# Routed experts of a fused attention and MoE kernel: late weight pieces behind evictions, early branch hints, gate products last, a third block's transposes inside the second's plan

## The chip, the cores and the metric

The kernel runs on one core of one Trainium2 chip. The metric is the device time of one launch in microseconds (us), the median of several runs. Each kernel is also profiled once; the times in the rows below are microseconds from the start of that profiled execution's span.

## The reference

Three stages follow each other on 1152 tokens (2 x 576) of 512 features:

1. Attention with 8 heads of 64 in which a token sees itself and the 63 before it.
2. A dense mixture of 4 experts: `out += p[:, e:e+1] * (relu(x @ w1[e]) @ w2[e])`, w1 512 x 1024, w2 1024 x 512.
3. A routed mixture of 8 experts, whose weights are other tensors. This is the stage that the change is about:

```python
skip_score = x @ w_skip
do_compute = skip_score > 0
out = x.copy()
xc = x[do_compute]
logits = xc @ w_gate
e_idx = np.argmax(logits, axis=1)
probs = np.exp(logits_s)
probs /= probs.sum(-1, keepdims=True) + 1e-09
gate_w = probs[np.arange(len(xc)), e_idx]
for e in range(E):
    mask = e_idx == e
    h = np.maximum(xc[mask] @ w1[e], 0.0)
    y[mask] = gate_w[mask, None] * (h @ w2[e])
out[do_compute] = xc + y
```

With the inputs used, 154 tokens are skipped, and experts 0 to 7 get 116, 207, 129, 66, 298, 17, 114 and 51. In blocks of 128 tokens: expert 0 has one; 1 has a second, full one; 2 has a second one with so few tokens that a small form (64 rows) serves; 3 has one; 4 has a full second and a small third one; 5 and 6 have one; 7 has a single small one.

## The kernel before, in words

Attention runs to about 90 us of the profile, the dense experts to about 488 us. Beside the last dense expert the routing is worked out tile by tile (nine tiles of 128 tokens, `route`, from L625 on): gate values, argmax, a running count, and products on PE (`tab`, L743) that collect each token's place, id and gate. From 488 us on the routed experts run one after the other, and the rest of this document is about them.

**An expert's block** (`block`, L885) works on 128 token rows. The rows are fetched from DRAM by an indirect DMA that POOL issues (`gather`, L851, tile `xg`; `xj` for a third block). `xpose` (L363 transposes on PE, then L878 on ACT and L880 on DVE) turns them and splits them into a high and a low part, `xs`. The first product (`g1`, two halves called g10 and g14 after their first chunk, matmuls L902) lands in PSUM as `mm`; in second and third blocks the PSUM tile is called `mmx`. ACT evicts it with the ReLU as `hr` (L926). PE transposes `hr` (L943), ACT and DVE split that into `ht` (L947, L950), and the second product (`g2`, L902 again) follows. DVE multiplies by the gate and adds to the token rows (L986, tile `xg`), and POOL scatters the rows to the output by an indirect DMA (`scatter`, L859). A `small` block does the same for 64 rows.

**Weights** come as eight pieces of 512 KB for each expert, four of w1 and four of w2, issued by SP (`w_load`, L315 for w1, L317 for w2) into a ring of `raw` buffers. ACT casts a piece to its high part (`wa1h`, `wa2h`, L331) and DVE subtracts for the low part (`wa1l`, `wa2l`, L335); the letters a and b are two sets of weight buffers used in turn, expert 0 having b and expert 1 having a. A raw buffer is free for the next load when both have read it.

**What sets the order.** The code does not issue instructions where it stands. `add(engine, duration, function, rd, wr, prio, slack)` gives an operation to `Plan`, and `plan.run()` sorts what has been collected: a list scheduler that walks along modelled times and takes, for each engine, the operation that is ready with the lowest `prio`; `slack` moves an operation's modelled readiness. The modelled times only set the order. On the chip every engine runs its own list in that order and waits at semaphores. So an operation that waits holds up all that stands behind it on its engine.

**Branches.** Counts are known only on the chip, so each expert's extra blocks stand behind branches, which every engine takes for itself: `more{e}` (L1105: are there more than one block?), the choice of the full or the small form (L1062), and the third block (L1095). Counters come into registers by three loads on each engine (`TENSOR_LOAD cnt x3`, L1052). On PE a hint (`ahead`, L1085) tells the sequencer ahead of time which way `more{e}` goes.

**Names that the steps use:** in `w_pass`, `w_split` of expert 1's w2; in `route`, `pick`, `rank` and `grab` (choice of the token rows of expert 0's first block, which come straight from SBUF by a product and not by a gather) and `spread` (the `tab` products); `route_gates`, which puts the gate products of the last tiles into the plan; `gather(e, 2)`, the rows of a third block; `rows` and `more`, which build the second and third blocks.

Of the kernel before, what the change touches and what calls it, by code (L numbers as in the profile page):

```python
# [204 lines left out]
def fused_kernel(ctx: ExitStack, tc: tile.TileContext, q, k, v, dp, w1, w2, wskip, wgate, m1, m2, out):  # L205
# [114 lines left out]
        add("X" if early else "SP", 0.0 if early else 1.46, f, rd=["M"] if extra else [], new=[b], prio=prio)  # L320
        return b

    def w_split(b, ring, key, part, c, prio, pool=False, after=(), hpool=False, hdve=False):
# [12 lines left out]

        add("POOL" if hpool else "DVE" if hdve else "ACT", 3.5 if hpool else c_dve(FF // 2) if hdve else c_act(FF, False), hi, rd=[b], wr=[(key, part, "h", c)], prio=prio)
# [285 lines left out]
    late, later = [], []  # L623

    def route(t):  # L625
        i = t % 2
        T = lambda nm: R[nm, i]
        K = lambda nm: ("r", nm, i)
        P = -5.0
        sl = 1.0 if t < TT - 1 else 0.0  # L630
        for d, nm in ((scr, "scr"), (out, "out")):
            add("SP", 0.8, lambda d=d: SP.dma_start(out=d[t * 128:(t + 1) * 128, :], in_=x2[:, t]),
# [77 lines left out]
            PE.matmul(out=first_at(kk), lhsT=x2[:, t, kk * 128:(kk + 1) * 128], rhs=rp.tile,  # L710
                      start=False, stop=(t == TT - 1), skip_group_check=True)

        if t > GT:
            rp = R["rpr"].buf()
            add("DVE", 0.35, pick, rd=["pf", K("oh"), "rconst"], new=[rp], prio=P)
        add("DVE", 0.2, rank, rd=["pf", K("oh")], wr=[K("ps")], prio=P + 0.5)
        if t > GT:
            for kk in range(KC):
                add("PE", 0.22, lambda kk=kk: grab(kk), rd=[rp, ("x2", t)], wr=[first[kk // 2]],
                    prio=P if t == TT - 1 else 3000.0)  # L720
            rp.close()

        def gate(c):
            sc, g, gb = T("sc"), T("g"), T("gb")
# [9 lines left out]
        def spread(c0, c1, pr, after=()):  # L734

            e0, n = c0 * E2, (c1 - c0) * E2
            wx = lambda: T("wy" if c0 else "wx")[:, :, 0:n]
            add("DVE", c_dve(TT * n) + 0.01, lambda: DVE.tensor_tensor(
                out=wx(),
                in0=T("w")[:, c0:c1].rearrange("p c e -> p (c e)").unsqueeze(1).to_broadcast([128, TT, n]),  # L740
                in1=T("oj").unsqueeze(2).to_broadcast([128, TT, n]), op=ALU.mult),
                rd=[K("oj")] + [K("w0")] * (c0 == 0) + [K("w1")] * (c1 == 5), wr=[K(("wx", c0))], prio=pr)
            add("PE", max(0.11, TT * n / 2400), lambda: PE.matmul(  # L743
                out=R["tab"].rearrange("p j c e -> p j (c e)")[:, :, e0:e0 + n], lhsT=T("r"), rhs=wx(),
                start=(t == 0), stop=(t in (GT, TT - 1)), skip_group_check=True),
                rd=[K("r"), K(("wx", c0)), *after], wr=[("tab", c) for c in range(c0, c1)], prio=pr, slack=sl)

        def gates(after=(), pr=2):
            for c in range(3):
# [2 lines left out]
        def weigh(after):  # L752
            add("DVE", 0.8, slot, rd=[K("ps"), *after], wr=[K("r"), K("oj")], prio=1)
            if t < TT - 2:
                gates()
                spread(0, 5, 2)
            else:
                spread(0, 2, 1)
                later.append(lambda: (gates(["idg", ("htl", 4)], 15), spread(2, 5, 15, ["idg"])))

        late.append(weigh)
        if t != TT - 2:
# [122 lines left out]
    def block(e, j, xg, x, small=False, amid=None):  # L885
# [46 lines left out]
        def tr(c0, w, hr):  # L932
            p = pt_r.buf()
            s = slice(c0, c0 + w)
            n = 64 if small else 128

            def turn():
                for g in range(w):
                    h = hr[:, 128 * g:128 * g + 128]
                    if small:  # L940
                        PE.matmul(out=p[:, g, 0:64], lhsT=h, rhs=fold2, start=True, stop=True)
                    else:
                        PE.transpose(out=p[:, g, :], in_=h, identity=ident)  # L943
# [6 lines left out]
            add("DVE", c_dve(w * n), lambda: DVE.scalar_tensor_tensor(  # L950
                out=ht[:, s, n:2 * n], in0=p[:, 0:w, 0:n], scalar=0.0, in1=f32(ht[:, s, 0:n]), op0=ALU.max,
                op1=ALU.subtract),
                rd=[p, ht, (ht, "h", c0)], wr=[(ht, "l", c0), ("htl", c0)], prio=-1)
            p.close()

        hrs = [g1(*pieces[0])]
# [37 lines left out]
    def w_pass(kd, e, p, prio=None):  # L994
        if prio is None:
            npass[0] += 1
            prio = 500.0 + 10 * npass[0]
        src = ((w1, w2) if kd == "m" else (m1, m2))[p - 1][e]
        ring, key = (wa, "wa") if kd == "m" else (rings[e], rkey[e % 2])
        for c in range(4):  # L1000
            extra = kd == "r" and e > 0 and p == 2
            st = KN["w2s"] if (kd, e, p) == ("m", 0, 2) else 2.5
            b = w_load(src, p, c, prio + st * c, extra, early=kd == "r" and e > 2 and p == 1)
            w_split(b, ring, key, p, c, prio + st * c, pool=(kd, e, p) == ("m", 0, 2) and KN["w2pool"][c],
                    after=["idg"] if kd == "r" and e == 1 else [])

    with tc.manual_schedule():
        w_pass("m", 0, 2, KN["w2p"])
        for e in range(E1):
# [28 lines left out]
            if e + 1 < E1:  # L1038
                w_pass("m", e + 1, 2)
        route_end()  # L1040
        add("X", 0.0, open_moe2, rd=["pf"], wr=["M"] + [("x2", t) for t in range(TT)] + [(x, f) for x in ("hh", "hl") for f in range(FC)], slack=-0.43)
        xgs, xts = {}, {}
        for j in range(2):
# [15 lines left out]
        def rows(e, j, x, xt):  # L1059

            state = [(b, b.left, b.closed) for b in (x, xt)], [(r, len(r.free)) for r in Ring.made]
            with tc.If(over(e, 2 * j + 1)) as c:  # L1062
                block(e, j, x, xt)
                if j == 0:
                    ahead(e)
                scatter(e, j, x)
                plan.run()
            with c.Else():
                for b, left, closed in state[0]:
                    b.left, b.closed = left, closed  # L1070
                for r, n in state[1]:
                    r.free = [0.0] * n
                block(e, j, x, xt, small=True)
                if j == 0:
                    ahead(e)
                scatter(e, j, x, 64)
                plan.run()

        def further(e):

            return nv[2] > 0 if e == E2 - 1 else over(e, 2)

        def hint(e):

            tc.mark_branch_hint_location(f"more{e}", hint=further(e), engines=[PE.engine, POOL.engine] if e == E2 - 1 else [PE.engine])  # L1085

        def ahead(e):
            if e:
                add("PE", 0.05, lambda: hint(e), rd=[("g2", 0)], wr=[("g2", 1)], prio=10.0)
            else:  # L1090
                add("PE", 0.05, lambda: hint(e), rd=["nv", ("g10", 1)], wr=[("g10", 2)], prio=10.0)

        def more(e, xt):
            for j in (1, 2):
                with tc.If(over(e, 4)) if j == 2 else ExitStack():  # L1095
                    if j == 2 and e == E2 - 1:
                        xgs[e, j] = gather(e, j)
                    if j == 2 or xt is None:
                        xt = xpose(xgs[e, j], 0)
                        plan.run()  # L1100
                    rows(e, j, xgs[e, j], xt)

        def tails(e, xt):

# [26 lines left out]

        for e in range(E2):
            last = e == E2 - 1
            if not last:
                xgs[e, 2] = gather(e, 2, 7, [("g2", 0)])
            if last:
                plan.run()
                rows(e, 0, xgs[e, 0], xts[e, 0])
                tails(e, None)
                continue  # L1140
            block(e, 0, xgs[e, 0], xts[e, 0], amid=None if e else route_gates)
            if e == 0:
                add("X", 0.0, counts, rd=["cnt"], wr=["nv"], slack=1.5)
            ahead(e)
# [43 lines left out]
```

## Time and profile before

| | us |
|---|---|
| median of 3 runs | 661.92 (660.07 to 665.22) |
| the profiled execution: its own time | 666.29 |
| the profiled execution: its span | 664.5 |
| PE busy | 631.3 (95% of the span) |
| DVE, ACT, POOL busy | 322.6, 235.9, 89.1 |

The mean granted clock of PE is 0.983 of full speed. PE is a matrix engine whose busy time is modelled from pipelined matmuls, so 95% is not 95% of its peak. The stage that the change touches begins at about 488 us. In the rows of the trace, a bracket at the end of a row is idle time of that engine just before the instruction and what released it; "issue" there is time in which the engine waited for nothing that the profile shows; PEq is PE's sequencer.

### The profile page before, as it was taken

To read this page: it belongs to the slowest core of one execution; us is meant where nothing else is said; L and a number is where in the kernel's file an instruction comes from. 1 tells how busy PE (TensorE), PEld (TensorE's weight loads), DVE (VectorE), ACT (ScalarE), POOL (GpSimd) and SP (SyncE) were. 2 spreads that over 40 slices of the span, in tenths; PEclk is the share of its full clock that TensorE was granted. 3 is DMA by queue.
4 is the path that set the end of the run, shared out by engine and by line. 5 is a ranking of instruction groups with operands and counts; after the bars stand their busy time and mean duration, and the time that the engine had idled before them with its cause. 6 is when DMAs were issued, how large, how long until landed. Compare 5 with 4: busy or idle time off the path is not lost. (4 is left out here: it accounts for less than half of the span.)

```text
span 664.5 us, 9657 instructions
## 1 busy us (share of the span) xinstructions
PE 631.3 (95%) x3652; PEld 556.0 (84%) x3652; DVE 322.6 (49%) x700; ACT 235.9 (36%) x492; POOL 89.1 (13%) x111
## 2 busy tenths in 40 slices
PE   7899999999999999999999999999968999999984
PEld 6787898898989898989898988989856878787764
DVE  5996841127412124412124426255657855862861
ACT  4974750125302013301013302113413764753741
POOL 6541130000000000000000000000023321320510
PEclk9998999999999999999999999999997999999988
DMA  9767200006400003400004401020538976990820
GB/s 218 163 160 224 47 4 0 1 1 211 169 1 0 1 1 126 127 1 0 1 1 127 127 32 65 14 83 12 191 122 309 314 228 215 295 332 19 245 100 11
DMA packets 55770, 71.40 MB, mean 107 GB/s; under 512 B 32938, under 2 KB 32938, under 8 KB 55697
## 3 DMA queue, kind: packets, MB, share of 16 engines
q1 hardware_dynamic: 52912, 62.17, 29.7%
q0 software_dynamic: 2784, 8.28, 4.0%
q8 instruction: 42, 0.69, 0.4%
q14 instruction: 32, 0.25, 0.1%
HBM read 63.74 MB, written 7.47 MB: 107 GB/s over the span
## 5 line engine op out<-in xcount | busy, mean ns | idle before, releaser
L523 PE MATMUL mm<-xth,wa1h 128*128 128x384 f32 (+1 forms) x416 | 138.0, 332 | 0.0
L523 PE MATMUL mm<-xtl,wa1h 128*128 128x384 f32 (+1 forms) x416 | 135.8, 326 | 0.0
L523 PE MATMUL mm<-xth,wa1l 128*128 128x384 f32 (+1 forms) x416 | 135.7, 326 | 0.0
L529 ACT ACTIVATE hh<-mm 128x384 fp32r<-128x384 f32 (+1 forms) x104 | 48.5, 467 | 236.3 <-PE mm L523 227.7
L544 PE MATMUL mm<-wa2h,hh 128*128 128x512 f32 (+1 forms) x296 | 116.8, 395 | 0.0
L544 PE MATMUL mm<-wa2h,hl 128*128 128x512 f32 (+1 forms) x296 | 115.0, 388 | 0.0
L544 PE MATMUL mm<-wa2l,hh 128*128 128x512 f32 (+1 forms) x296 | 114.9, 388 | 0.0
L531 DVE SCALAR_TENSOR_TENSOR hl<-mm,hh 128x384 fp32r<-128x384 f32 (+1 forms) x104 | 54.5, 525 | 123.2 <-ACT hh L529 123.2
L523 PEld LDWEIGHTS mm<-xth,wa1h 128*128 128x128 f32 x416 | 78.9, 190 | 0.7
L523 PEld LDWEIGHTS mm<-xtl,wa1h 128*128 128x128 f32 x416 | 78.8, 189 | 0.5
L523 PEld LDWEIGHTS mm<-xth,wa1l 128*128 128x128 f32 x416 | 78.7, 189 | 0.0
L544 PEld LDWEIGHTS mm<-wa2h,hl 128*128 128x128 f32 x296 | 55.7, 188 | 12.3
L544 PEld LDWEIGHTS mm<-wa2l,hh 128*128 128x128 f32 x296 | 55.8, 189 | 11.0
L544 PEld LDWEIGHTS mm<-wa2h,hh 128*128 128x128 f32 x296 | 55.8, 188 | 11.0
L556 DVE SCALAR_TENSOR_TENSOR x<-mm,prob,x 128x512 f32<-128x512 f32 (+1 forms) x28 | 20.5, 732 | 91.3 <-PE mm L544 91.3
L767 POOL DMA_INDIRECT x<-scr,id x1 | 1.3, 1252 | 360.2 <-DVE id L784 360.2
L331 ACT CAST wa2h<-raw 128x1024 fp32r<-128x1024 f32 x32 | 33.2, 1048 | 29.0 <-PE mm L544 18.6
L335 DVE TENSOR_TENSOR wa1l<-raw,wa1h 128x1024 fp32r<-128x1024 f32 x31 | 36.6, 1219 | 4.4 <-ACT wa1h L331 2.0
L335 DVE TENSOR_TENSOR wa2l<-raw,wa2h 128x1024 fp32r<-128x1024 f32 x30 | 35.9, 1218 | 5.2 <-ACT wa2h L331 5.0
L331 ACT CAST wa1h<-raw 128x1024 fp32r<-128x1024 f32 x30 | 30.0, 1049 | 13.0 <-DMA raw<-in_moe_w_dram 5.1
L950 DVE SCALAR_TENSOR_TENSOR ht<-pt,ht 128x512 fp32r<-128x512 f32 (+2 forms) x27 | 15.1, 569 | 31.3 <-ACT ht L947 27.6
L444 POOL TENSOR_TENSOR s<-s,mx 128x512 f32<-128x512 f32 x18 | 20.2, 1122 | 51.7 <-DVE mx L441 40.5
(206 smaller groups left out, 921.2 us busy)
## 6 DMA issues: line engine op xcount, KB each, us to landing
raw<-in_moe_w_dram SPq DMA_DIRECT2D x96, 512.0 KB, 5.5
scr<-x SPq DMA_DIRECT2D x9, 256.0 KB, 2.1
out_dram<-x SPq DMA_DIRECT2D x9, 256.0 KB, 2.3
qn<-in_q_dram SPq DMA_DIRECT2D x8, 256.0 KB, 4.0
kn<-in_k_dram SPq DMA_DIRECT2D x8, 256.0 KB, 3.9
vn<-in_v_dram SPq DMA_DIRECT2D x8, 256.0 KB, 4.7
qn<-in_q_dram SPq DMA_DIRECT2D x2, 128.0 KB, 4.6
kn<-in_k_dram SPq DMA_DIRECT2D x2, 128.0 KB, 4.7
```

Of the source, the lines that this page charges most:

```text
L331: (POOL.tensor_copy if hpool else DVE.tensor_copy if hdve else ACT.copy)(out=aps()[0], in_=b.tile)
L335: (POOL if pool else DVE).tensor_tensor(out=l, in0=b.tile, in1=f32(h), op=ALU.subtract)
L444: add("POOL", 1.0, lambda: POOL.tensor_tensor(out=s.tile, in0=s.tile, in1=mx[:, 3].unsqueeze(2).to_broadcast([128, HP, 128]), op=ALU.mult) ...
L523: PE.matmul(out=ps[:, 0:n], lhsT=wa[a][:, kk, f * 128:(f + 1) * 128], rhs=x[:, kk, g0:g0 + n], start=(i == 0), stop=(i == 3 * KC - 1))
L529: add("ACT", c_act(n), lambda: ACT.activation(out=hh[:, f, 0:n], in_=ps[:, 0:n], func=ACTF.Relu), rd=[ps], wr=[("hh", f)], prio=-1)
L531: add("DVE", c_dve(n), lambda: DVE.scalar_tensor_tensor(out=hl[:, f, 0:n], in0=ps[:, 0:n], scalar=0.0, in1=f32(hh[:, f, 0:n]), op0=ALU.max ...
L544: PE.matmul(out=ps[:, 0:c1 - c0], lhsT=x[:, f, o:o + 128], rhs=wa[a][:, f, c0:c1], start=(f == 0 and i == 0), stop=(f == FC - 1 and i == 2))
L556: DVE.scalar_tensor_tensor(out=z, in0=y, scalar=prob[:, t, e:e + 1], in1=z, op0=ALU.mult, op1=ALU.add)
L767: add("POOL", 1.0, lambda: POOL.indirect_dma_start(out=R["x0"], out_offset=None, in_=scr[0:128 * (GT + 1), :], in_offset=bass.IndirectOffs ...
L950: add("DVE", c_dve(w * n), lambda: DVE.scalar_tensor_tensor(out=ht[:, s, n:2 * n], in0=p[:, 0:w, 0:n], scalar=0.0, in1=f32(ht[:, s, 0:n]), ...
```

## The change

Four parts, all in the routed stage and what leads to it.

1. Expert 1's w2 pieces get `slack=7.0` on ACT, and the low parts of its w1 no longer have to follow the routing's index table (`idg`); only those of w2 do.
2. The choice of token rows of the next to last tile is put after the last tile's rows are there (`mid`), the gate products of the routing have no longer to follow a part of expert 0's block (`htl`) but get PE priority 21, and `route_gates` is called after `route_end` and not from inside expert 0's block.
3. `ahead`: the hint of every expert now follows the second group of g10; before, only expert 0's did, and the others' followed the first group of g2. In expert 1's and later blocks it stands 38 rows ahead of the branch on PE; before, 13.
4. The third block's rows are gathered after the first block's next gathers, and its transposes are put into the plan of the full second block (`amid`, prio 11.5); the branch to the third block stands inside that of the second's full form.

```diff
-    def w_split(..., hdve=False):
+    def w_split(..., hdve=False, slack=0.0):
...
-        add(... "ACT" ..., hi, rd=[b], wr=[(key, part, "h", c)], prio=prio)
+        add(... "ACT" ..., hi, rd=[b], wr=[(key, part, "h", c)], prio=prio, slack=slack)
...
+        while mid:
+            mid.pop()([("x2", t)])
...
-        if t > GT:
-            rp = R["rpr"].buf()
-            add("DVE", 0.35, pick, rd=["pf", K("oh"), "rconst"], new=[rp], prio=P)
-        add("DVE", 0.2, rank, rd=["pf", K("oh")], wr=[K("ps")], prio=P + 0.5)
...
+        def choose(after=()):
...
+        if t == TT - 2:
+            mid.append(choose)
+        else:
+            choose()
...
-                rd=[K("r"), K(("wx", c0)), *after], wr=[("tab", c) for c in range(c0, c1)], prio=pr, slack=sl)
+                rd=[K("r"), K(("wx", c0)), *after], wr=[("tab", c) for c in range(c0, c1)], prio=pe or pr, slack=sl)
...
-                later.append(lambda: (gates(["idg", ("htl", 4)], 15), spread(2, 5, 15, ["idg"])))
+                later.append(lambda: (gates(["idg"], 15), spread(2, 5, 15, ["idg"], 21)))
...
-                    after=["idg"] if kd == "r" and e == 1 else [])
+                    after=["idg"] if kd == "r" and e == 1 and p == 2 else [], slack=7.0 if kd == "r" and e == 1 and p == 2 else 0.0)
...
         route_end()
+        route_gates()
...
+            def gathered():
+                if e == E2 - 1:
+                    xgs[e, 2] = gather(e, 2)
+                third["xt"] = xpose(xgs[e, 2], 11.5)
             with tc.If(over(e, 2 * j + 1)) as c:
-                block(e, j, x, xt)
+                block(e, j, x, xt, amid=gathered if j == 1 else None)
...
                 plan.run()
+                if j == 1:
+                    with tc.If(over(e, 4)):
+                        rows(e, 2, xgs[e, 2], third["xt"])
...
         def ahead(e):
-            if e:
-                add("PE", 0.05, lambda: hint(e), rd=[("g2", 0)], wr=[("g2", 1)], prio=10.0)
-            else:
-                add("PE", 0.05, lambda: hint(e), rd=["nv", ("g10", 1)], wr=[("g10", 2)], prio=10.0)
+            add("PE", 0.05, lambda: tc.mark_branch_hint_location(f"more{e}", hint=further(e), engines=[PE.engine]),
+                rd=[("g10", 1)] + ["nv"] * (e == 0), wr=[("g10", 2)], prio=10.0)
...
-            for j in (1, 2):
-                with tc.If(over(e, 4)) if j == 2 else ExitStack():
...
+            if xt is None:
+                xt = xpose(xgs[e, 1], 0)
+                plan.run()
+            rows(e, 1, xgs[e, 1], xt)
...
-            if not last:
-                xgs[e, 2] = gather(e, 2, 7, [("g2", 0)])
...
-            block(e, 0, xgs[e, 0], xts[e, 0], amid=None if e else route_gates)
+            block(e, 0, xgs[e, 0], xts[e, 0])
+            xgs[e, 2] = gather(e, 2, 7, [("g2", 0)])
```

Line numbers of the changed kernel are higher by 10 from `block` on (L902 is L912, L926 is L936), and the branches' lines are L1120 (`more`), L1080 (full or small) and L1087 (third block).

How the order of instructions moves at three places:

On ACT, in expert 0's block, before; L926 evicts expert 0's hidden rows, `wa2h` casts are those of expert 1's w2.

```order
L878 CAST xs<-mm 128x256
L331 CAST wa2h<-raw_4175 128x1024
L926 ACTIVATE hr<-mm 128x512
L331 CAST wa2h<-raw_4195 128x1024
L1052 TENSOR_LOAD cnt x3
L947 ACTIVATE ht<-pt 128x4x128
L926 ACTIVATE hr<-mm 128x512
L331 CAST wa2h<-raw_4209 128x1024
L947 ACTIVATE ht<-pt 128x4x128
L331 CAST wa2h<-raw_4228 128x1024
L878 CAST xs<-pt 128x512 x2
```

The same place on ACT after the change:

```order
L888 CAST xs<-mm 128x256
L936 ACTIVATE hr<-mm 128x512
L1063 TENSOR_LOAD cnt x3
L957 ACTIVATE ht<-pt 128x4x128
L936 ACTIVATE hr<-mm 128x512
L957 ACTIVATE ht<-pt 128x4x128
L331 CAST wa2h<-raw_4180 128x1024
L888 CAST xs<-pt 128x512 x2
L331 CAST wa2h<-raw_4199 128x1024
L331 CAST wa2h<-raw_4212 128x1024
L331 CAST wa2h<-raw_4231 128x1024
```

The two evictions and the two `ht` parts, which stood behind one to three casts, now stand ahead of all four.

On POOL, expert 1's first block, before: gathers for later blocks (`xg`), for a third block (`xj`), the scatter and the branch `more`.

```order
L851 DMA xj<-scr,idg 128x512
L851 DMA xg<-scr,idg 128x512 x2
L859 DMA out_dram<-xg,ids 1152x512
L1105 REGISTER_ALU
L1105 COMPARE_AND_BRANCH
```

And after the change:

```order
L861 DMA xg<-scr,idg 128x512 x2
L861 DMA xj<-scr,idg 128x512
L869 DMA out_dram<-xg,ids 1152x512
L1120 REGISTER_ALU
L1120 COMPARE_AND_BRANCH
```

The third block's gather has moved from the first place to the third; so it has in the blocks of experts 2 to 6, while expert 0's order (six `xg`, then `xj`) stays.

On PE, from the end of expert 1's first block into its second, before (third-block transposes stand ahead of the third block, behind the branch of L1095):

```order
L902 MATMUL mm<-wa2h,ht 128x512 x4
L1105 REGISTER_ALU
L1105 COMPARE_AND_BRANCH
L1062 REGISTER_ALU
L1062 COMPARE_AND_BRANCH
L902 MATMUL mmx<-wa1h,xs 128x512
L902 MATMUL mmx<-wa1l,xs 128x512
L902 MATMUL mmx<-wa1h,xs 128x512
L902 MATMUL mmx<-wa1l,xs 128x512
L902 MATMUL mmx<-wa1h,xs 128x512
```

And after:

```order
L912 MATMUL mm<-wa2h,ht 128x512 x4
L1120 REGISTER_ALU
L1120 COMPARE_AND_BRANCH
L1080 REGISTER_ALU
L1080 COMPARE_AND_BRANCH
L912 MATMUL mmx<-wa1h,xs 128x512
L912 MATMUL mmx<-wa1l,xs 128x512
L912 MATMUL mmx<-wa1h,xs 128x512
L912 MATMUL mmx<-wa1l,xs 128x512
L363 MATMUL pt<-ident,xj 128x128 x4
L912 MATMUL mmx<-wa1h,xs 128x512
```

The four transposes of `xj` now stand behind the fourth matmul of the full second block, in every expert that has one.

## Rows read from the trace of the kernel before

**Rows 1.** Waits of PE, 488 to 664 us: total us, times, longest us.

```profile
PE pt L943 <- ACT hr L926: 5.5, 2, 4.8
PE mm L902 <- DVE wa2l L335: 2.9, 1, 2.9
PE mm L902 <- PEq L1105: 1.7, 2, 0.9
```

**Rows 2.** Windows around gaps of PE: length, then busy time of each engine.

```profile
core 0: us, PE busy (x) PEld busy (x) DVE busy (x) ACT busy (x) POOL busy (x), PEclk, DMA share, GB/s
...
493.55:498.38 4.83, 0.01 (x1) 0.01 (x1) 1.23 (x1) 1.60 (x3) 3.59 (x3) 1.00 0.96 311
498.56:505.39 6.83, 6.14 (x19) 4.65 (x19) 3.63 (x5) 4.36 (x6) 4.63 (x4) 0.50 1.00 361
600.58:602.82 2.24, 0.73 (x6) 0.42 (x5) 1.44 (x2) 0.61 (x1) 0.88 (x1) 1.00 0.00 0
639.74:642.74 3.00, 0.15 (x2) 0.04 (x1) 2.82 (x3) 0.00 (x0) 1.74 (x1) 0.86 0.03 8
642.74:648.75 6.01, 6.01 (x20) 5.27 (x21) 0.20 (x1) 0.98 (x2) 0.00 (x0) 0.50 0.12 42
```

**Rows 3.** PE's timeline in expert 0's block: start, us, instruction, idle before.

```profile
498.38 1.02 PE L943 MATMUL pt<-ident,hr 128*128 128x128 f32 x4 [4.83 <-ACT hr L926]
...
510.97 1.09 PE L902 MATMUL mm<-wb2h,ht 128*128 128x512 f32 x4
512.21 0.47 PE L902 MATMUL mm<-wa1h,xs 128*128 128x512 f32 x1
```

**Rows 4.** ACT's timeline in expert 0's block.

```profile
496.78 1.04 ACT L331 CAST wa2h<-raw 128x1024 fp32r<-128x1024 f32 x1 [8.19 <-DMA raw<-in_moe_w_dram]
```

**Rows 5.** DVE's timeline behind its three counter loads.

```profile
495.11 1.23 DVE L335 TENSOR_TENSOR wa1l<-raw,wa1h 128x1024 fp32r<-128x1024 f32 x1 [1.77 <-issue]
```

**Rows 6.** POOL's timeline: gathers and scatters, experts 0, 1, 3 and 4.

```profile
494.18 0.96 POOL L851 DMA_INDIRECT xg<-scr,idg  x1 [33.49 <-DVE idg L796]
495.45 1.70 POOL L851 DMA_INDIRECT xg<-scr,idg  x1 [0.30 <-issue]
497.45 0.95 POOL L851 DMA_INDIRECT xg<-scr,idg  x1 [0.31 <-issue]
...
513.64 1.75 POOL L859 DMA_INDIRECT out_dram<-xg,ids  x1 [9.39 <-DVE xg L986]
...
519.62 1.37 POOL L851 DMA_INDIRECT xg<-scr,idg  x1 [0.55 <-DMA out_dram<-xg,ids]
521.29 0.95 POOL L851 DMA_INDIRECT xg<-scr,idg  x1 [0.30 <-issue]
...
575.53 1.74 POOL L859 DMA_INDIRECT out_dram<-xg,ids  x1 [6.83 <-DVE xg L986]
...
582.43 0.94 POOL L851 DMA_INDIRECT xg<-scr,idg  x1 [2.60 <-DMA out_dram<-xg,ids]
```

**Rows 7.** DMA issues of 494.18; 495.45 and 521.29; 582.43 and 497.45; 632.74: landing us.

```profile
xg<-scr,idg POOLq DMA_INDIRECT x1, 7.4
...
xg<-scr,idg POOLq DMA_INDIRECT x1, 7.6
...
xg<-scr,idg POOLq DMA_INDIRECT x1, 8.3
...
xj<-scr,idg POOLq DMA_INDIRECT x1, 4.5
```

**Rows 8.** PE's timeline: first matmuls of the second blocks, experts 1 and 4.

```profile
525.37 0.40 PE L902 MATMUL mmx<-wa1h,xs 128*128 128x512 f32 x1
...
588.69 0.39 PE L902 MATMUL mmx<-wb1h,xs 128*128 128x512 f32 x1
```

**Rows 9.** PE's timeline: first matmul of expert 4.

```profile
575.40 0.49 PE L902 MATMUL mm<-wb1h,xs 128*128 128x512 f32 x1 [0.94 <-PEq L1105]
```

**Rows 10.** DVE's timeline: the last rows before expert 7 begins on PE.

```profile
640.59 2.35 DVE L335 TENSOR_TENSOR wa2l<-raw,wa2h 128x1024 fp32r<-128x1024 f32 x2
```

More of the change, by code (lines that the diff above doesn't have):

```diff
@@ L321, in w_load, with w_split @@
         return b
-    def w_split(b, ring, key, part, c, prio, pool=False, after=(), hpool=False, hdve=False):
+    def w_split(b, ring, key, part, c, prio, pool=False, after=(), hpool=False, hdve=False, slack=0.0):
         def aps():
@@ L335, in lo @@
             (POOL if pool else DVE).tensor_tensor(out=l, in0=b.tile, in1=f32(h), op=ALU.subtract)
-        add("POOL" if hpool else "DVE" if hdve else "ACT", 3.5 if hpool else c_dve(FF // 2) if hdve else c_act(FF, False), hi, rd=[b], wr=[(key, part, "h", c)], prio=prio)
+        add("POOL" if hpool else "DVE" if hdve else "ACT", 3.5 if hpool else c_dve(FF // 2) if hdve else c_act(FF, False), hi, rd=[b], wr=[(key, part, "h", c)], prio=prio, slack=slack)
         if pool:
@@ L621, in route_loads @@
         SP.dma_start(out=R["wr"][:, :, E2], in_=wskip.rearrange("(k p) -> p k", p=128))
-    late, later = [], []
+    late, later, mid = [], [], []
     def route(t):
@@ L711, in grab @@
                       start=False, stop=(t == TT - 1), skip_group_check=True)
-        if t > GT:
-            rp = R["rpr"].buf()
-            add("DVE", 0.35, pick, rd=["pf", K("oh"), "rconst"], new=[rp], prio=P)
-        add("DVE", 0.2, rank, rd=["pf", K("oh")], wr=[K("ps")], prio=P + 0.5)
[L717 to L721, printed above, removed]
+        def choose(after=()):
+            nonlocal rp
+            if t > GT:
+                rp = R["rpr"].buf()
+                add("DVE", 0.35, pick, rd=["pf", K("oh"), "rconst", *after], new=[rp], prio=P)
+            add("DVE", 0.2, rank, rd=["pf", K("oh"), *after], wr=[K("ps")], prio=P + 0.5)
+            if t > GT:
+                for kk in range(KC):
+                    add("PE", 0.22, lambda kk=kk: grab(kk), rd=[rp, ("x2", t)], wr=[first[kk // 2]],
+                        prio=P if t == TT - 1 else 3000.0)
+                rp.close()
+        rp = None
+        if t == TT - 2:
+            mid.append(choose)
+        else:
+            choose()
         def gate(c):
@@ L732, in gate, with spread @@
                 DVE.tensor_tensor(out=g[:, c + 1:c + 2], in0=g[:, c:c + 1], in1=gb[:, c:c + 1], op=ALU.subtract)
-        def spread(c0, c1, pr, after=()):
+        def spread(c0, c1, pr, after=(), pe=None):
             e0, n = c0 * E2, (c1 - c0) * E2
@@ L952, in tr @@
                 op1=ALU.subtract),
-                rd=[p, ht, (ht, "h", c0)], wr=[(ht, "l", c0), ("htl", c0)], prio=-1)
+                rd=[p, ht, (ht, "h", c0)], wr=[(ht, "l", c0)], prio=-1)
             p.close()
@@ L1061, in rows @@
             state = [(b, b.left, b.closed) for b in (x, xt)], [(r, len(r.free)) for r in Ring.made]
+            third = {}
+            def gathered():
+                if e == E2 - 1:
+                    xgs[e, 2] = gather(e, 2)
+                third["xt"] = xpose(xgs[e, 2], 11.5)
             with tc.If(over(e, 2 * j + 1)) as c:
-                block(e, j, x, xt)
+                block(e, j, x, xt, amid=gathered if j == 1 else None)
                 if j == 0:
@@ L1077, in rows @@
                 plan.run()
+            if j == 1:
+                M["xj"].free = [0.0] * M["xj"].n
         def further(e):
             return nv[2] > 0 if e == E2 - 1 else over(e, 2)
-        def hint(e):
-            tc.mark_branch_hint_location(f"more{e}", hint=further(e), engines=[PE.engine, POOL.engine] if e == E2 - 1 else [PE.engine])
         def ahead(e):
-            if e:
-                add("PE", 0.05, lambda: hint(e), rd=[("g2", 0)], wr=[("g2", 1)], prio=10.0)
-            else:
-                add("PE", 0.05, lambda: hint(e), rd=["nv", ("g10", 1)], wr=[("g10", 2)], prio=10.0)
+            add("PE", 0.05, lambda: tc.mark_branch_hint_location(f"more{e}", hint=further(e), engines=[PE.engine]),
+                rd=[("g10", 1)] + ["nv"] * (e == 0), wr=[("g10", 2)], prio=10.0)
         def more(e, xt):
-            for j in (1, 2):
-                with tc.If(over(e, 4)) if j == 2 else ExitStack():
[L1096 to L1101, printed above, removed]
+            if xt is None:
+                xt = xpose(xgs[e, 1], 0)
+                plan.run()
+            rows(e, 1, xgs[e, 1], xt)
         def tails(e, xt):
```

## The prediction

> **What bounds the kernel now.** I read the page first: PE is busy for 631.3 us of the 664.5 us span, so only time in which PE stands still, or runs at the lower clock, can be won. Then I asked for PE's waits in the routed part alone, 488 to 664 us [rows 1]. Three items matter: 5.5 us for hidden rows that ACT evicts (one wait of 4.8), 2.9 us put down to a DVE pass, 1.7 us for PE's own sequencer at the branch to an expert's second block. Third, a table of those stretches [rows 2]. [...] At half the clock a stretch in which PE is busy throughout (6.01 of 6.01) does what takes half as long at the full one, so it gives away about 3.0 us.
>
> The profiled execution took 666.29 us (span 664.5 and 1.8 around it), 4.4 above the median of 661.92. I add the differences below, worked out inside it, to the median.
>
> **Expert 0's block: ACT's order.** The 4.83 us gap ends with PE's transposes at 498.38 [rows 3]; they wait for hr, which ACT evicts behind a cast that itself stood 8.19 us for a weight transfer and ran from 496.78 on [rows 4]. The eviction had nothing else to wait for: PE's own work ended at 493.55 [rows 2]. After the change it runs at once. Expert 1 begins at 512.21 now [rows 3]. What goes: the 4.83 gap, about 3.3 us of lower clock behind it, and the second wait for hr, 5.5 - 4.8 = 0.7 [rows 1]: together 8.8.
> What comes instead: the three reads of counters on PE, which the long gap covers today, stand free (0 at best; DVE's wait at the same three reads is 1.77 [rows 5]; I take 1.5, near that row). And the eight transposes of gathered rows (xg) stand before the last matmuls of g2. PE would reach them at about 500.2, but the first two gathers are issued at 494.18 and 495.45 [rows 6] and take 7.4 and 7.6 us to land [rows 7]: 501.6 and 503.05. A new wait of 2.9 us, in two pieces. The last xg transposes, two gate products, eight matmuls of g2 and the branch are left: 2.65 (from 510.97 to 512.21, [rows 3], go the last four matmuls and the branch, 1.24; the rest I set at 1.4 by that row's pace, 1.09 for four). Expert 1 begins at 503.05 + 2.65 = 505.7, **6.5 earlier**. Nothing reaches higher, since the gathers' issue does not move. The low end: w1 raw buffers come free earlier, so SP issues up to 1.5 MB more in this stretch; at the 361 GB/s of [rows 2] that is 4.2 us of traffic, and if all of it came ahead of the gathers, the gain would be 2.3. I take 6.5, since gathers later in the program, with loads around them, still take 7.6 to 8.3 [rows 7].
> [...]
>
> **Expert 1: the third block's transposes.** Expert 1 has 207 tokens: two blocks, no third one. PE now meets four transposes of xj after four matmuls of the second block, whether or not a third follows. The chain up to xj is POOL's: scatter of expert 0's first block, its landing (which frees xg's buffer), two xg gathers, then xj, third where it was first. Today the scatter is issued at 513.64, 1.4 after expert 1 begins, and the first gather behind it at 519.62 [rows 6], 6.0 later. After: scatter at about 507.4 (its own rows land at about 505.7, then a DVE pass), gathers at 513.4 and 515.1, xj at 516.3, landed at 523.9 with the 7.6 of [rows 7]. PE is there at 505.7 + 13.2 (512.21 to 525.37, [rows 3, 8]) + 0.9 = 519.8. It stands for **4.1 us**, and its fifth matmul comes at about 524.6 instead of 526.3. Of the 6.5 only 1.7 is left. Bounds: with the shortest gather in the trace, 4.5 us [rows 7], the wait is 1.0; with 8.3 it is 4.8. I take 7.6, a gather of this very pair. A gap of 4.1 us is nearer to 4.83 and 3.00 than to 2.24, so I charge a lower stretch, 3.0 us (0 to 3.4).
>
> **Expert 4.** Here the second block is full and the third is real. The gap of 2.24 us between them, with transposes and splits [rows 2], goes. But the same chain decides: the scatter of expert 3 is issued at 575.53, the first xg gather at 582.43, when it has landed [rows 6]; the second and xj follow at 1.27 us each (as 494.18 and 495.45 do), 584.97, and xj lands 8.3 later [rows 7], at 593.27. PE is there at 588.69 + 0.9 = 589.6 [rows 8]: a wait of 3.7, and with the transposes (0.5) the fifth matmul comes 4.2 later than now. Net **+2.0**, and once more 3.0 for the clock (gap 4.2). With a gather of 4.5 there would be no wait and a gain of 1.6. The matmuls behind are PE-bound, so nothing gives this back.
>
> **Hints and branches.** The hint goes from 13 rows ahead of its branch to 38. Expert 0's hint already stood about 32 ahead, and behind it PE goes from 512.06 to 512.21 without a wait [rows 3]; with a late one the wait is 0.94 [rows 9], the other of [rows 1] 0.8. Of the two, the one before expert 4 is swallowed by expert 4's chain, which the scatter sets (0); the one before expert 6 gives **0.6**. Before expert 7 PE jumps twice in a gap of 3.00 us, to 642.74 [rows 2]. The waits put it down to DVE's wa2l [rows 1], but the passes of that name end at 640.59 + 2.35 = 642.94 [rows 10], 0.2 after PE has started, and expert 7's first matmul doesn't read wa2l. I take it for the jumps: **0.8** off, a gap of 2.2, and like the 2.24 one no lower clock behind it: **3.0** (0 if it stays). One branch fewer behind a small second block and one jump more behind the third cancel; each is bounded by the 0.94 of [rows 9].
>
> **Sum:** -1.7 + 3.0 (expert 1) + 2.0 + 3.0 (expert 4) - 0.6 - 0.8 - 3.0 = +1.9: 668.2 for the profiled execution, **664** for the median. The trace can tell some 1% (7 us; the three runs spread over 5).
>
> **Rivals.**
> B, the gathers of xj come in time: for it speaks the 4.5 us of one xj gather; against it that all gathers in a group of three took 7.4 to 8.3. Then expert 1's wait is 1.0 and without lower clock: -6.5 + 1.0 + 0.6 = -4.9; expert 4 gains 1.6 and keeps the 0.8 of its hint; with -0.6 - 0.8 - 3.0 that is -11.7: 650.
> C, slower: the earlier loads of w1 do get in the way of the first two gathers. At 361 GB/s for at most 1.5 MB they land up to 4.2 later; with 3.8, the stand before the xg transposes grows from 2.9 to 6.7, longer than the gap that brought the lower clock, and everything behind, expert 1's chain too, moves with it: +1.9 + 3.8 + 3.0 = +8.7: 671. It decides from 1.7 us of delay on if the clock falls there (1.9 + 1.7 + 3.0 = 6.6, 1%), from 4.7 if not. For it: the DMA share is already 1.00 in that stretch [rows 2].
> D, the early hints do nothing: the gaps at branches stay, the 0.6, 0.8 and 3.0 are not won, 1.9 + 4.4 = +6.3: 668. For it speaks that the target lies far off and many instructions are fetched in between; against it expert 0's early hint, with a wait of 0.
> [...]
>
> **Chances.** My forecast, with its own range of 657 (no clock drops: -4.1) to 668: 0.36. B 0.28, C 0.24, D 0.12. A and D lie within 1%: same 0.48; faster 0.28; slower 0.24. The range takes in most of B and C: 651 to 671.
>
> **What would show it.** Right: PE's transposes of expert 0 close behind the matmuls, the next wait naming the xg gathers; in expert 1 and 4 a wait of some 4 us four matmuls into the second block, released by the landing of xj, with 0.50 of the clock behind it; expert 1 beginning 6 to 7 us earlier; no wait above 0.3 at the branches. Wrong: no wait at xj's transposes (B), gathers of over 9 us in expert 0's block (C), waits for PE's sequencer as before (D), or the full clock behind the new gaps, which alone would bring 6 us.

## The result, and the profile after

| kernel | median us | ratio to before (95% interval) |
|---|---|---|
| before | 662.03 (660.07 to 665.22) | |
| changed | 669.98 | 1.0109 (1.0079 to 1.0139) |

The change makes the kernel 0.8 to 1.4% slower, 7 to 8 us. One of the four runs of the changed kernel took 1242.5 us; it counts in the median of 669.98 and not in the ratio, and without it the median is 669.57. 664 was forecast with a range of 651 to 671: the range holds the time and the side of the likeliest case was right, but its size was some 6 us short. Whether the change stays within the 1% that the likeliest case gave is not settled: the interval lies across that line.

PE's waits in the routed part of the changed kernel (total us, times, longest) show another list than [rows 1]:

```profile
PE pt L363 <- DMA xj<-scr,idg: 12.0, 2, 7.3
PE pt L363 <- DMA xg<-scr,idg: 2.5, 2, 2.1
PE pt L953 <- DVE ht L960: 1.7, 2, 0.9
PE mm L912 <- DVE xg L996: 0.9, 1, 0.9
```

The 5.5 us for hr, the 2.9 before expert 7 and the 1.7 for PE's sequencer at `more` are gone. In their place stand 12.0 us in two waits for the landing of xj, the third block's rows. PE's timeline has them four matmuls into the second block of expert 1 and of expert 4:

```profile
506.93 0.48 PE L912 MATMUL mm<-wa1h,xs 128*128 128x512 f32 x1
...
520.40 0.40 PE L912 MATMUL mmx<-wa1h,xs 128*128 128x512 f32 x1
...
526.17 1.09 PE L363 MATMUL pt<-ident,xj 128*128 128x128 f32 x4 [4.67 <-DMA xj<-scr,idg]
...
539.90 0.50 PE L912 MATMUL mm<-wb1h,xs 128*128 128x512 f32 x1 [0.43 <-PEq L1087]
...
575.79 0.49 PE L912 MATMUL mm<-wb1h,xs 128*128 128x512 f32 x1
...
589.88 0.39 PE L912 MATMUL mmx<-wb1h,xs 128*128 128x512 f32 x1
598.26 1.08 PE L363 MATMUL pt<-ident,xj 128*128 128x128 f32 x4 [7.29 <-DMA xj<-scr,idg]
...
620.66 0.39 PE L912 MATMUL mm<-wa1h,xs 128*128 128x512 f32 x1
...
649.05 0.47 PE L912 MATMUL mm<-wa1h,xs 128*128 128x512 f32 x1 [0.88 <-DVE xg L996]
```

A table of stretches of the same kernel (columns as in [rows 2]) has the granted clock around the two waits and behind the wait for xg in expert 0's block:

```profile
526.17:529.40 3.23, 3.23 (x10) 2.75 (x11) 0.69 (x1) 0.62 (x1) 0.00 (x0) 0.50 1.02 399
...
598.26:601.50 3.24, 3.24 (x11) 2.77 (x12) 0.69 (x1) 0.62 (x1) 0.00 (x0) 0.56 0.39 149
...
502.88:506.00 3.12, 3.12 (x12) 2.65 (x13) 1.98 (x5) 2.26 (x4) 0.00 (x0) 0.58 1.03 404
...
649.05:653.00 3.95, 3.95 (x26) 3.59 (x26) 2.17 (x2) 0.98 (x2) 1.74 (x1) 1.00 0.18 65
```

The clock falls behind both waits for xj, as forecast, but comes back after some 3 us of work (3.23 us at 0.50, 3.24 us at a mean of 0.56; 1.00 from 529.5 and 601.5 us on). Behind the first wait 128x512 matmuls began 0.42 to 0.43 us apart at 0.50 (527.49, 527.91, 528.34) and 0.23 apart at 1.00 (530.46, 530.69, 530.92): by these numbers the two stretches cost an estimated 1.5 us each, not 3.0. Behind the shorter gap before expert 7 the clock stays at 1.00.

POOL's timeline holds the cause of the two waits. The first four rows belong to expert 0's scatter and what follows it, the others to experts 2 and 3:

```profile
507.85 1.75 POOL L869 DMA_INDIRECT out_dram<-xg,ids  x1 [5.19 <-DVE xg L996]
514.95 1.39 POOL L861 DMA_INDIRECT xg<-scr,idg  x1 [5.35 <-DMA out_dram<-xg,ids]
516.64 0.95 POOL L861 DMA_INDIRECT xg<-scr,idg  x1 [0.30 <-issue]
517.89 1.17 POOL L861 DMA_INDIRECT xj<-scr,idg  x1 [0.30 <-PE pt L363]
...
564.53 5.07 POOL L869 DMA_INDIRECT out_dram<-xg,ids  x1 [8.63 <-DVE xg L996]
569.90 0.98 POOL L861 DMA_INDIRECT xg<-scr,idg  x1 [0.30 <-issue]
575.01 1.18 POOL L861 DMA_INDIRECT xg<-scr,idg  x1 [4.13 <-DVE xs L890]
576.50 1.88 POOL L861 DMA_INDIRECT xj<-scr,idg  x1 [0.31 <-issue]
578.68 1.02 POOL L869 DMA_INDIRECT out_dram<-xg,ids  x1 [0.30 <-issue]
586.89 1.40 POOL L861 DMA_INDIRECT xg<-scr,idg  x1 [7.18 <-DMA out_dram<-xg,ids]
588.60 0.95 POOL L861 DMA_INDIRECT xg<-scr,idg  x1 [0.30 <-issue]
589.85 0.95 POOL L861 DMA_INDIRECT xj<-scr,idg  x1 [0.30 <-issue]
```

In expert 1 the chain is the predicted one, 1.6 us later: scatter at 507.85, xg at 514.95 when it has landed, xj at 517.89; it lands 8.2 us after the start of its issue. In expert 4 an earlier link is late: the issue of expert 2's last scatter takes 5.07 us where the same issue took 0.94 us in the first profile of before. Behind it the second xg gather waits until 575.01. Its row names a DVE pass, which ended at 574.23, but the scatter landed then too, 9.7 us after 564.53; with that scatter quicker the same gather is released by its landing (the run with DVE's passes spread, below). Expert 3's scatter, ready when DVE's pass ended at 576.43 (575.68 and 0.75), is queued behind that gather and xj until 578.68; before, it went out at 575.53 [rows 6]. DVE's row:

```profile
575.68 0.75 DVE L996 SCALAR_TENSOR_TENSOR xg<-mm,gates,xg 128x512 f32<-128x512 f32 x1 [0.31 <-PE mm L912]
```

### The profile page after: what moved, and what is told of

It reads as the page before. It is cut to its first block, busy times and chain, and to the rows that moved or that the text cites. A ratio compares the mean times of both kernels' runs of the same rounds, so it can differ in the third digit from the quotient of the medians.

```text
span 667.8 us, 9678 instructions
## 1 busy us (share of the span) xinstructions
PE 629.9 (94%) x3656; PEld 555.4 (83%) x3656; DVE 323.0 (48%) x701; ACT 237.4 (36%) x493; POOL 89.4 (13%) x111
## 5 line engine op out<-in xcount | busy, mean ns | idle before, releaser
L869 POOL DMA_INDIRECT out_dram<-xg,ids x11 | 19.4, 1768 | 84.7 <-DVE xg L996 67.2
```

Source lines behind the costliest of these rows:

```text
L869: add("POOL", 1.0, lambda: POOL.indirect_dma_start(out=out, out_offset=bass.IndirectOffsetOnAxis(ap=R["ids"][0:n, j, e:e + 1], axis=0), in ...
```

## The experiments

Each ratio is to runs of the kernel before made beside that kernel, with medians of 661.60, 662.77 or 662.80 us.

| kernel | median us | ratio to before (95% interval) |
|---|---|---|
| changed, without part 4 | 653.54 | 0.9876 (0.9835 to 0.9916) |
| before, part 4 alone | 672.78 | 1.0150 (1.0108 to 1.0192) |
| changed, gather of xj first | 657.33 | 0.9931 (0.9906 to 0.9956) |
| changed, transposes of xj later | 655.66 | 0.9900 (0.9865 to 0.9935) |
| changed, both of these | 653.07 | 0.9858 (0.9820 to 0.9897) |
| changed, DVE passes spread | 663.63 | 1.0026 (1.0001 to 1.0052) |
| before, parts 1 and 2 | 656.29 | 0.9920 (0.9893 to 0.9948) |
| before, part 1 alone | 658.12 | 0.9926 (0.9899 to 0.9952) |
| before, part 2 alone | 659.35 | 0.9938 (0.9914 to 0.9962) |
| before, part 3 alone | 660.85 | 0.9977 (0.9957 to 0.9997) |
| before, once more | 662.65 | |

**Is it part 4?** First the changed kernel without it, then part 4 alone on the kernel before.

```diff
-                block(e, j, x, xt, amid=gathered if j == 1 else None)
+                block(e, j, x, xt)
...
-            rows(e, 1, xgs[e, 1], xt)
+            for j in (1, 2):
+                with tc.If(over(e, 4)) if j == 2 else ExitStack():
```

> The changed kernel without its fourth part: the third block's rows are gathered and transposed as before (own gather first, transposes behind the third block's branch); slack, gate products and early hints stay. Theory (the loss is the two waits of PE for the landing of xj, 4.67 us in expert 1 and 7.29 us in expert 4, and the stretch of half clock behind each): both waits are gone, expert 1 begins at about 507 us of the profile, its second block runs through; 651 to 655 us against 662 of before. Rival 1 (the earlier loads and the other order on ACT and POOL cost it, not the transposes): 661 us or more. Rival 2 (the early hints lose what the first parts win): waits for PE's sequencer of 0.7 to 1.1 us before experts 4, 6 and 7.

> The kernel before with the fourth part of the change alone. Theory: PE waits for xj after four matmuls of the second block, 3 to 5 us in expert 1 and 3 to 7 us in expert 4, with half clock behind each for about 5 us; the 2.24 us gap between second and third block goes; 668 to 674 us. Rival 1 (other parts cost it): within 2 us of 662.

653.54 and 672.78: both times are as the theory has them, and rival 1 is out. Without part 4 there is no wait for xj at all, none for PE's sequencer at `more` either (rival 2 is out), and the other three parts are worth 1.2%. Part 4 alone costs 1.5%. Of its two waits the one in expert 1 is longer than the 3 to 5 us expected, 5.87, and the one in expert 4 is 2.99; PE's waits in that kernel:

```profile
PE pt L363 <- DMA xj<-scr,idg: 8.9, 2, 5.9
PE pt L943 <- ACT hr L926: 4.6, 1, 4.6
PE mm L902 <- PEq L1113: 2.4, 3, 1.1
```

**Is it the wait or the transposes?** One line is moved, so that POOL issues xj first; or one number is changed, so that PE comes to the transposes later; or both.

```diff
+            xgs[e, 2] = gather(e, 2, 7, [("g2", 0)])
             block(e, 0, xgs[e, 0], xts[e, 0])
-            xgs[e, 2] = gather(e, 2, 7, [("g2", 0)])
```

> The changed kernel with one line moved: the gather of the third block's rows is put into the plan ahead of the block again, so that POOL issues xj before the two xg gathers and not behind them; the transposes stay after the fourth matmul of the second block. Theory (the wait is for a gather that stands in POOL's queue behind gathers that wait for a scatter's landing): xj is issued about 6 us earlier in expert 1 and 10 us earlier in expert 4, both waits fall below 1 us, no half clock behind them, 651 to 656 us. Rival 3 (transposes inside the second block and the nested branch cost by themselves): within 3 us of the changed kernel's 670.

```diff
-                third["xt"] = xpose(xgs[e, 2], 11.5)
+                third["xt"] = xpose(xgs[e, 2], 19.5)
```

> The changed kernel with one number changed: priority 19.5 in place of 11.5 for the third block's transposes, so that they stand some 5.4 us into the full second block and not 0.9. The gather of xj stays third in POOL's order. Theory (PE is early for a late gather): the wait in expert 1 falls from 4.67 to 0.5 us at most, the half clock behind it goes; in expert 4 about 3 us of 7.3 are left; 656 to 661 us. Rival 3 (transposes in the second block and the nested branch cost by themselves): within 3 us of 670.

> Both: the gather of xj ahead of the xg gathers and the transposes 5.4 us into the second block. Theory: no wait for xj in either place; 654 to 658 us if the gap before expert 7 is 3 us with half clock behind it, as with the gather moved alone; 651 to 654 us if that gap is 0.9 us. The third block's transposes in the second block are then worth about 1 us against the changed kernel without its fourth part (653.5 us, gap before expert 7 of 0.89 us).

All three beat both kernels, so rival 3 is out: the transposes inside the second block cost next to nothing when their rows have landed. With xj first PE finds them there in both places, with no idle time ahead of them, and the four take 0.60 us:

```profile
519.31 0.60 PE L363 MATMUL pt<-ident,xj 128*128 128x128 f32 x4
...
582.40 0.60 PE L363 MATMUL pt<-ident,xj 128*128 128x128 f32 x4
...
634.00 0.77 PE L912 MATMUL mm<-wa1h,xs 128*128 128x512 f32 x1 [3.04 <-issue]
```

It missed its expected range by 1.3 us; the last of these rows has a gap of 3.04 us before expert 7, half clock behind it (0.50 from 634 to 638 us). With the transposes late and the gather third, expert 1 doesn't wait, and expert 4 still waits 2.44 us; 655.66 is 0.3 under what was expected. Both together, 653.07, do as well as the kernel without part 4 (653.54); their intervals overlap, so what part 4 is worth in its best form isn't settled. By the two profiles it wins 2.5 us between the beginnings of experts 2 and 5 (71.83 against 74.37), and 1.6 are lost up to expert 1's beginning (19.26 against 17.66, counted from the first matmul of expert 0's block).

**Why 7.29 us in expert 4?** The slow issue of 5.07 us lies beside four passes of DVE, here in DVE's timeline of the changed kernel:

```profile
564.17 4.62 DVE L335 TENSOR_TENSOR wb1l<-raw,wb1h 128x1024 fp32r<-128x1024 f32 x4
```

They begin 0.36 us ahead of the scatter's issue at 564.53 and end at 568.79, the issue at 569.60. In the first profile of before the same four passes began at 563.12, 0.5 us after that scatter (562.62), and its issue took 0.94 us. The experiment gives these four passes a slack, which moves them apart.

```diff
-            add("DVE", c_dve(FF), lo, ..., prio=prio)
+            add("DVE", c_dve(FF), lo, ..., prio=prio, slack=late)
...
+                    late=4.0 if kd == "r" and e == 4 and p == 1 else 0.0
```

> The changed kernel with one slack more: the four DVE passes for the low parts of expert 4's w1 no longer stand together at the start of expert 3's block but one by one between its other DVE work. Theory (expert 4's wait for xj is 7.3 us and not 3.7 because POOL's issue of expert 2's last scatter takes 5.07 us beside these four passes, and all gathers and scatters behind it are late): that issue takes about 1 us, the second xg gather behind it comes at about 571 us and not 575, expert 3's scatter at 576.5 and not 578.7, and expert 4's wait for xj falls to 3.5 to 5.5 us; 666 to 669 us. Rival (the 5.07 us have another cause, such as a full descriptor ring): 5.07 us again, the same wait of 7 us, 670 us.

POOL's and PE's timelines of that kernel:

```profile
563.29 0.94 POOL L869 DMA_INDIRECT out_dram<-xg,ids  x1 [8.63 <-DVE xg L996]
564.53 0.97 POOL L861 DMA_INDIRECT xg<-scr,idg  x1 [0.30 <-issue]
566.35 0.96 POOL L861 DMA_INDIRECT xg<-scr,idg  x1 [0.85 <-DMA out_dram<-xg,ids]
...
575.48 1.74 POOL L869 DMA_INDIRECT out_dram<-xg,ids  x1 [6.91 <-DVE xg L996]
```

```profile
574.55 0.48 PE L912 MATMUL mm<-wb1h,xs 128*128 128x512 f32 x1
...
592.02 0.39 PE L912 MATMUL mmx<-wb1h,xs 128*128 128x512 f32 x1
593.64 0.63 PE L363 MATMUL pt<-ident,xj 128*128 128x128 f32 x4 [0.53 <-DMA xj<-scr,idg]
```

The issue takes 0.94 us, and everything behind it follows at once: without the DVE passes beside it there is no delay, and the rival, another cause alone, is out. That the passes are not enough by themselves is said below. The wait falls further than expected, to 0.53. Half of that is PE coming later: the spread passes make expert 4's first block longer (592.02 - 574.55 = 17.5 us against 589.88 - 575.79 = 14.1). The time is 6 us less all the same, 2.4 under the expected range.

**What are the other parts worth?** Parts 1 and 2 together, each alone, then part 3.

```diff
-                    after=["idg"] if kd == "r" and e == 1 else [])
+                    after=["idg"] if kd == "r" and e == 1 and p == 2 else [], slack=7.0 if kd == "r" and e == 1 and p == 2 else 0.0)
```

> The kernel before with the first two parts alone: evictions ahead of the casts on ACT, choice and gate products later, route_gates early; late hints and the third block as before. Theory: expert 1 begins at about 507 us, 5 us earlier, and nothing gives it back: 656 to 658 us. Rival 1 (earlier w1 loads slow the gathers, or the order hurts later): 661 us or more, with gathers of over 9 us or a wait of PE for xg above 4 us.

> The kernel before with the first part alone: the slack of expert 1's w2 casts and the earlier low parts of its w1. Theory: this part carries the front's gain: no wait of 4.8 us for hr, expert 1 begins 3 to 6 us earlier, 656 to 659 us. Rival (the gate products hold PE up without the second part): within 2 us of 662.

> The kernel before with the second part alone: choice of the rows after the last tile, gate products last, route_gates early. Theory: the wait of 4.7 us for hr stays, since the casts stand ahead of the eviction as before; within 2 us of 662. Rival (the order of gate products carries the gain): 660 us or less.

Together and part 1 alone as expected. Part 2 alone was a miss: the wait for hr was to stay, and 3.4 us are gained. PE's timeline shows the reason:

```profile
493.82 0.50 PE L912 MATMUL mm<-wb1h,xs 128*128 128x512 f32 x1 [1.51 <-issue]
498.76 0.66 PE L953 MATMUL pt<-ident,hr 128*128 128x128 f32 x4 [2.82 <-ACT hr L936]
506.23 0.48 PE L912 MATMUL mm<-wa1h,xs 128*128 128x512 f32 x1
```

The matmuls of the next chunk now stand ahead of the transposes, so PE waits in two pieces, 1.51 and 2.82 us, and every microsecond from 488 to 514 has the full clock (1.00); in the kernel before one gap (4.65 us in its second profile, 4.83 in the first) is followed by a half-clock stretch (0.50 up to 503 and up to 505 us). Expert 1 begins 18.55 us after the first matmul of expert 0's block, where it is 23.75 in the second profile of before. The two parts attack the same gap, so their gains don't add.

```diff
-                add("PE", 0.05, lambda: hint(e), rd=[("g2", 0)], wr=[("g2", 1)], prio=10.0)
+            add("PE", 0.05, ..., rd=[("g10", 1)] + ["nv"] * (e == 0), wr=[("g10", 2)], prio=10.0)
```

> The kernel before with the third part alone: every hint after the second group of g10. Theory: the waits for PE's sequencer before experts 4 and 6 (0.94 and 0.76 us) go, expert 4's is not swallowed since xj is not waited for; 1.5 to 2 us less: 659.5 to 660.5 us, and about 655 to 657 if the gap before expert 7 shrinks to 0.9 us with them. Theory of code placement: the gap of 3.0 us before expert 7 is a fetch of instructions (a packet in the instruction queues inside the gap) that the hint does not reach, so it stays 2.5 to 3.1 us, as it did in the kernel with the gather moved. Rival 2 (an early hint is lost): the waits before experts 4 and 6 stay at 0.7 to 1.1 us, 662 us.

Rival 2 is out: experts 4 and 6 begin without a wait for the sequencer. So is the theory of code placement as put there: the gap before expert 7 is 0.89 us. But the median, 660.85, is only 0.03 to 0.43% below before and not at the 655 to 657 given for that case. Part of it goes again to a wait that is new in that kernel, for DVE's low part of ht in the first blocks of experts 4 and 6, in PE's list of waits:

```profile
PE pt L943 <- DVE ht L950: 1.7, 2, 0.9
```

Another 0.81 us goes to a wait for ACT's cast `wb1h` in expert 1's first block. The rest of the difference stays open.

**How far is one profile from another?**

> The kernel before, unchanged, once more with a profile. The same gap of 2.5 to 3.1 us before expert 7 with a packet of the instruction queues in it. If half clock follows the gap again, it belongs to the kernel; if not, the 3.0 us that the first profile shows there are not in every execution, and part of the 4.4 us between the first profile and the median is explained.

The second profile of the kernel before took 662.65, near the median; half clock follows the gap before expert 7 again (expert 7's first matmul took 0.77 us there, as it did in the first profile at 0.50; expert 5's took 0.39). Its routed part is 1.5 us shorter than in the first profile, and the part ahead of it 2.1 us. PE's timeline, for the account below:

```profile
486.23 0.51 PE L902 MATMUL mm<-wb1h,xs 128*128 128x512 f32 x1 [0.47 <-ACT xs L878]
...
509.98 0.47 PE L902 MATMUL mm<-wa1h,xs 128*128 128x512 f32 x1
...
535.85 0.51 PE L902 MATMUL mm<-wb1h,xs 128*128 128x512 f32 x1 [0.44 <-PEq L1095]
...
573.73 0.48 PE L902 MATMUL mm<-wb1h,xs 128*128 128x512 f32 x1 [1.47 <-PEq L1105]
...
610.43 0.39 PE L902 MATMUL mm<-wa1h,xs 128*128 128x512 f32 x1
...
640.38 0.77 PE L902 MATMUL mm<-wa1h,xs 128*128 128x512 f32 x1 [2.45 <-DVE wa2l L335]
```

## Why the prediction was right or wrong

Against that second profile, counted from the first matmul of expert 0's block (488.05 in the changed kernel, 486.23 before), the changed kernel stands so:

| point | before | changed | difference | forecast |
|---|---|---|---|---|
| expert 1 begins | 23.75 | 18.88 | -4.9 | -6.5 |
| expert 2 begins | 49.62 | 51.85 | +2.2 | +1.3 |
| expert 4 begins | 87.50 | 87.74 | +0.2 | not given |
| expert 5 begins | 124.20 | 132.61 | +8.4 | +6.3 |
| expert 7 begins | 154.15 | 161.00 | +6.9 | +4.9 |
| end of the span | 174.67 | 179.75 | +5.1 | +1.9 |

The rest, up to the 7 to 8 us of the runs, lies ahead of this stage (1.8 us in these two profiles, where the first matmul of the stage came at 486.2 to 488.4 us in all profiles of this study) and in the scatter of single executions. Against the first profile of before, in which the forecast was worked out and whose routed part was 1.5 us longer, the end stands at +3.6.

That the range holds the time is in part luck. Its upper end of 671 was rival C's time, and C did not come about; the forecast's own range ended at 668. Two wrong terms also offset each other, the wait in expert 4 and the price of the clock (points 3 and 4).

1. **Expert 0's block: right in its mechanism, 1.6 us too good.** The new bound is the landing of the first two gathers, which take 7.7 and 7.6 us, where they took 7.4 and 7.6; the wait is 2.5 us (2.07 and 0.39) against 2.9. What the step left out is the half clock behind it, 3.1 us long at 0.58. The three reads of counters stood free for 0.67 us, not 1.5. The step's two reckonings did not agree either: what goes less what comes, 8.8 - 1.5 - 2.9, is 4.4, and its 6.5 follows from the landing alone. That nothing reaches higher isn't so: without part 4 the gate products stand ahead of the xg transposes, PE doesn't wait for xg at all, and expert 1 begins at 17.66 in the table's count, 1.2 us earlier. Rival C didn't come: SP's loads of w1 were issued in one go at 496.49, and the two gathers that PE waits for did not get slower. The five gathers behind those two did get slower, 8.5 to 9.2 us against 6.9 to 8.3; one passed the 9 us named as a sign of C, but PE didn't wait for it.
2. **Expert 1's transposes: right.** A wait of 4.67 us against 4.1, at the matmul that was named, by the chain that was named. The bounds of that step rest on a wrong reading: the gathers in groups of three took 6.1 to 9.9 us in the trace of before, not 7.4 to 8.3. The 8.2 that came lies within both. Rival B's condition, a gather that is there in time, is what the moved line brings about.
3. **Expert 4: the term that was mis-sized.** The working took expert 3's scatter to stay where it was, at 575.53. It went out at 578.68, 3.2 us later, since expert 2's last scatter took 5.07 us to issue; from there to the first gather behind it went 8.2 us, not 6.9. The wait became 7.29 us and not 3.7. That the order on one engine can move another engine's work beside a scatter was not in the step.
4. **The clock: right in kind, too dear.** The two gaps did bring the lower clock (0.50, and 0.56 in the mean), at an estimated 1.5 us each and not 3.0. The 3.0 was the author's estimate from 6.01 us at 0.50 in [rows 2]. That takes back 3.0 of the 3.6 that step 3 missed.
5. **Hints and branches: right, and rival D is out.** Expert 4 begins at 575.79 without a wait in its row. What D was argued from, instructions fetched in between, is there: one packet (0.02 MB) in the instruction queues from 565 us up to that start. The gap before expert 7 is 0.88 us (2.2 forecast, 2.45 in the second profile of before), with the full clock behind it; that gives 1.6 and, from there to the end, 1.8, together 3.3 where 3.8 were forecast. 0.85 of it goes again to a wait for ht in expert 6's block, and as much in expert 4's, which was not foreseen.

So it is the sum's size that missed: +1.9 forecast in the frame of the first profile, +5.1 in this one. By the differences of the table, expert 0's block is worse than forecast by 1.6, the way from expert 2 to expert 5 by 1.2 (a longer wait, a cheaper clock) and the end by 1.2; expert 1's blocks are better by 0.7. Between experts 2 and 4 the branches do give 2.0, but they only bring PE earlier to a wait whose end POOL sets, as the forecast had it.

## What to carry to other kernels

When work is put ahead of a branch, or deeper into a queue, follow its operands back to the queue that issues them: four transposes of 0.60 us together brought 12 us of waits, because their gather had gone from the first to the third place in POOL's order, behind two that wait for a scatter to land. The whole change with the gather left in front, or the transposes 5 us later, or both, beats the kernel before by 0.7 to 1.4%; without its fourth part it is 1.2%, so moving the transposes was shown to cost nothing then, not to gain. And cutting a long wait in two can be worth more than it takes off the wait: with part 2 alone PE waits 1.51 and 2.82 us in place of 4.65 and 0.7, 1.0 us less, and expert 1 begins 5.2 us earlier; PE's busy time up to there falls from 17.51 to 14.07 us, since its clock is the full one (1.00) throughout.

## What the runs showed of the hardware that was not expected

**POOL's issue of a scatter was held up beside DVE passes.** Beside four adjoining DVE passes of 1.16 us over 128x1024 floats the issue of a 64-row scatter took 5.07 us, without them 0.94; it ended 0.8 us after the last of them. The kernel before has it too, at 614.38 in POOL's timeline, beside passes at 614.02 to 618.64:

```profile
614.38 5.06 POOL L859 DMA_INDIRECT out_dram<-xj,ids  x1 [11.43 <-DVE xj L986]
```

and in DVE's timeline:

```profile
614.02 4.62 DVE L335 TENSOR_TENSOR wb1l<-raw,wb1h 128x1024 fp32r<-128x1024 f32 x4
```

Moving the passes away from expert 2's scatter took its delay away. But the passes alone don't make it. In the changed kernel the scatter of expert 4's third block, also of 64 rows, began 0.35 us after the first of four such passes, as expert 2's did (0.36), and took 1.65 us, in POOL's timeline

```profile
622.66 1.65 POOL L869 DMA_INDIRECT out_dram<-xj,ids  x1 [9.29 <-DVE xj L996]
```

and in DVE's:

```profile
622.31 4.62 DVE L335 TENSOR_TENSOR wb1l<-raw,wb1h 128x1024 fp32r<-128x1024 f32 x4
```

What else it takes is open, and by what mechanism the passes delay an issue was not shown. In both slow cases the issue ended not behind one pass but 0.8 us after all four (569.60 against 568.79, 619.44 against 618.64).

**The gap before expert 7 goes with packets in the instruction queues.** In the six profiles with a gap of 2.4 to 3.1 us there (before twice, its variants with part 1, 2 or 4 alone, and the changed one with the gather moved), a packet in each of the two instruction queues lies inside the gap (in the second profile of before the first of them 0.1 us ahead of it), here of the last of them:

```profile
q8 instruction: 1, 0.02, 1.9%
q14 instruction: 1, 0.01, 0.7%
```

In the kernel with parts 1 and 2, whose gap is 1.83 us, only the second is there; in the six with gaps of 0.9 to 1.4 us, the changed kernel among them, neither. All of these six have the early hints; but the kernel with the gather moved has them as well and still has both packets. So the early hint goes with the short gap in six of seven kernels. What decides the seventh is open; where the code lies was not tried. That the packets make the gap was not shown. Nor is an early hint lost in experts 4 and 6: both begin without a wait for PE's sequencer in the changed kernel (575.79 and 633.93) and in the one with part 3 alone (573.37 and 624.50).

**A gap's length alone doesn't tell whether the clock falls.** It fell behind gaps of 2.07, 4.67 and 7.29 us in the changed kernel and not behind 2.24 [rows 2] (1.00 from 602.82 to 609 us) or 2.82 us (1.00 from 499 to 514 us, part 2 alone). At one place, the second four xg transposes of expert 0's block, two kernels differ: with the transposes of xj late they took 1.09 us behind waits of 1.88 and 0.37 us, as they did in the changed kernel at half clock; with DVE's passes spread they took 0.63 behind 2.27 and 0.55 us. The stretch at half clock was 3.1 to 3.2 us long in the changed kernel and 6.0 to 6.8 us before [rows 2].
